# Banks of a skipped branch, its prefetch hint, and the order of the last routed rows

## The chip, the cores and the metric

The kernel runs on one core of a Trainium2 chip. The metric is the device time of one execution, in microseconds (us). Engine names: PE is the matrix engine (TensorE), PEld its weight loads, DVE is VectorE, ACT is ScalarE, POOL is GpSimd, SP is SyncE, which here does nothing but start DMA transfers. An engine takes its instructions in order; engines wait for each other through semaphores.

## The reference

Three parts follow each other: a clustered attention, a mixture of experts, and a bilinear block.

```python
# attention: B, H, S, D = 2, 8, 768, 64; 16 clusters per head
mask = q_assign[:, :, :, None] == k_assign[:, :, None, :]
scores = np.where(mask, scale * np.matmul(q, k.transpose(0, 1, 3, 2)), -1e9)
attn = softmax(scores)                       # over the last axis
x = (attn @ v) as 1536 rows of 512
# mixture of experts: 8 experts, each row goes to the one with the largest logit
expert_idx = np.argmax(logits, axis=1)
for e in range(E):
    h = np.maximum(x[mask] @ w1[e], 0.0)     # 512 -> 1024
    out[mask] = gate_w[mask, None] * (h @ w2[e])
# bilinear
out = ((out @ w_a) * (out @ w_b)) @ w_out    # 512 -> 1536 -> 512
```

## The kernel before

Everything is float32. A product of full precision is made of three passes over numbers split into a high and a low part (`hi`, `lo`): hi by hi, lo by hi, hi by lo. The expert weights come from memory in loads of 512 KB (`raw_0`, `raw_1`, ... on SP, L129, four buffers); ACT writes the high part of each half (L150), DVE the low part (L156), and only when both halves of a buffer are split may SP load into it again.

**Attention.** A loop over 96 steps (`for s in range(nst)`, L753) makes scores, row maxima, exponentials, transposes and the product with v. When a group of rows is done, `route_gen` (L600) finds for each row the expert and its place in that expert's list, and POOL scatters the row into the buffer `xs_d` in memory (L641), 256 places (CAP) for each expert. The work of a group is a generator whose parts are run between the steps.

**The near rows.** The last three tiles of rows (128 each) of the second batch would reach memory too late for expert 0, which is computed first. So expert 0's transposed input `xT_near`, two PSUM tiles, is put together on PE: `near_load` (L676) reads what memory holds of expert 0 into `xe_near`, `near_trans` (L682) transposes that by products with a unit matrix, and `inject(t)` (L688) adds the rows of tile t by 8 products with `oneh`, a matrix of ones and zeros that puts each row in its place (4 column groups, high and low part each). `near_hi` on ACT and `near_lo` on POOL split the rows. Before, the order on PE is inject(0), the place numbers `pos` of the last tile, inject(1), near_trans, the counts `cnt_p`, inject(2). Then ACT and DVE split the result into `xTh` and `xTl` (L901, L903).

**The experts.** From L1171 on a loop runs over steps G. Step G multiplies by a 128-column slice of w1 (`layer1`, 12 products into the PSUM tile `h_G`, which lies in the tag `et0` or `et1` by turns); ACT and DVE make `hh_G` and `hl_G` of it (L1063, L1064); two steps later `layer2(G)` (L1079) multiplies them by w2 into the two tiles `y`: 6 products. In PE's queue that reads h_0, h_1, then the branch below, then h_2, y of 0, h_3, y of 1, h_4, y of 2, and so on. h_G may only start when `hl_(G-2)` has been read out of the same PSUM tag. At f == 5 of each expert PE also transposes the next expert's rows (`trans_x`, L982).

**The branch.** If an expert has more than 256 rows, a branch (`rare`, L1004) computes the others. With these inputs no expert does, so all five engines skip it: each reads the largest count `most` (L1005), compares (L1006), and goes on behind the branch. So that semaphore counts are the same on both ways, the skipped way holds instructions that raise semaphores by what the branch would have (shown as EVENT_SEMAPHORE at L1006). What the branch reads and writes counts as a dependence: `ov_ph` and `ov_py` in it lie in the PSUM tags `et0` and `et1` and are read by DVE, so that h_2 behind it, in `et0`, waits for DVE's semaphore as it stands behind the branch. ACT's first work behind the branch is to start the load of expert 1's rows (`load_xe(1)`, L976), which waits for DMA semaphores that SP raises behind the branch. DVE computes, between the count and the branch, ten small operations on the counts (`ov_s`, `scan`, `ov_i`, L909 to L925), which the branch and later steps read.

L838 marks a place at which a hint for the branch is given, on PE. The program's order is fixed by hand (`manual_schedule`).

Of the kernel before, what the change touches and what calls it, by code (L numbers as in the profile page):

```python
# [9 lines left out]
F32 = mybir.dt.float32  # L10
# [12 lines left out]
P = 128  # L23
# [18 lines left out]
def kernel(  # L42
# [557 lines left out]
    def route_gen(b, t0, n):  # L600
# [10 lines left out]
        if near and t0 > HALF:  # L611
            inject(1)
            near_trans()
        sl = rt.tile([P, HALF, NE], F32, tag="r_sl", name=f"sl_{b}_{t0}", bufs=2)[:, :n]
# [66 lines left out]

    def near_trans():  # L682
        for j in range(DC):
            for t in range(CT):
                nc.tensor.matmul(near_t["ps"][j // 2][:, j % 2, t * P:(t + 1) * P], near_t["xe"][:, t, j * P:(j + 1) * P], ident,
                                 start=False, stop=False)

    def inject(t):  # L688

        if t == 0:  # L690
            near_t["ps"] = [psa.tile([P, 2, CAP], F32, tag="sc", name=f"xT_near_{u}", bufs=2) for u in range(2)]
        for j in range(DC):
            for k_ in ("hi", "lo"):
                nc.tensor.matmul(near_t["ps"][j // 2][:, j % 2, :], near_t[k_][:, t, j * P:(j + 1) * P], near_t["oneh"][:, t, :],
                                 start=(t == 0 and j % 2 == 0 and k_ == "hi"), stop=(t == HALF - 1 and j % 2 == 1 and k_ == "lo"))

# [56 lines left out]
    for s in range(nst):  # L753
# [44 lines left out]
        if pp == NP - 1:  # L798

            if i in (0, 2, 4, 6):  # L800
                split_some(1)
            if 8 <= i < 8 + HALF:
                near_hi(i - 8, 1, 0, 2 * (HP - 1) * D)
                near_lo(nc.gpsimd, i - 8, 1, 0, 2 * (HP - 1) * D)
        if s + 1 == nst or steps[s + 1][0] != g_:
            def then(g=g_):
                pp, t0, n = g
                b, hp = divmod(pp, HP)
                if hp < HP - 1:
                    yield from pv_gen(g)  # L810
                elif pp < NP - 1:
                    yield from pv_gen(g)
                    yield from pick_gen(b, t0, n)
                    yield
                    yield
                    yield from route_gen(b, t0, n)
                elif s + 1 < nst:
                    yield from pv_gen(g, pick_gen(b, t0, n))
                    yield from route_gen(b, t0, n)
                else:  # L820
                    yield from pv_gen(g, pick_gen(b, t0, n), lambda: inject(0))
                    near_hi(HALF - 1, 1, 2 * hp * D, DM)
                    yield from route_gen(b, t0, n)
            work.append(then())
        came = [(g, next(g, 0)) for g in work]
        later = [g for g, r in came if r is True]
        work = [g for g, r in came if r is None]

    work = (later + work)[::-1]
# [7 lines left out]
    inject(HALF - 1)  # L837
    tc.mark_branch_hint_location("rare", "LikelyTaken", engines=[mybir.EngineType.PE])  # L838
    for t in range(NT - HALF + 1, NT):
# [62 lines left out]
    for u in range(2):  # L902
# [5 lines left out]
    ov_s = left.tile([1, NE, OVM], F32, name="ov_s")  # L908
    nc.vector.tensor_tensor(out=ov_s, in0=cnt[0:1].to_broadcast([1, NE, OVM]),  # L909
                            in1=ovt.rearrange("p (o j) -> p o j", o=1).to_broadcast([1, NE, OVM]), op=ALU.is_gt)  # L910

    scan = [left.tile([P, 3 * NE], F32, name=f"scan_{i}") for i in range(2)]
    for t in scan:
        nc.gpsimd.memset(t, 0.0)
    nc.vector.tensor_scalar(out=scan[0][:, NE + 1:2 * NE + 1], in0=cnt[:, :, 0], scalar1=-float(CAP), scalar2=0.0, op0=ALU.add, op1=ALU.max)
    nc.vector.tensor_scalar(out=scan[0][:, 2 * NE + 1:], in0=cnt[:, :NE - 1, 0], scalar1=float(CAP), scalar2=None, op0=ALU.min)
    for i, d in enumerate((1, 2, 4, 8)):
        nc.vector.tensor_add(scan[1 - i % 2][:, NE:], scan[i % 2][:, NE:], scan[i % 2][:, NE - d:3 * NE - d])
    obase, pbase = scan[0][:, NE:2 * NE], scan[0][:, 2 * NE:]

    ov_i = left.tile([1, 4 * NE], I32, name="ov_i")
    nc.vector.tensor_copy(ov_i[:, :2 * NE], scan[0][0:1, NE:])
    with nc.allow_low_precision(reason="whole numbers below 2^24"):
        nc.vector.tensor_reduce(out=ov_i[:, 2 * NE:3 * NE], in_=ov_s, axis=AX.X, op=ALU.add)
    nc.vector.tensor_copy(ov_i[:, 3 * NE:], cnt[0:1, :, 0])  # L925

    psa_stack.close()
    ps_s = ctx.enter_context(tc.tile_pool(name="ps_s", bufs=2 * CT, space=PSUM, reuse_waits="tile"))
    ps_t = ctx.enter_context(tc.tile_pool(name="ps_t", bufs=1, space=PSUM, reuse_waits="tile"))
# [74 lines left out]
    def rare():  # L1004
        n_most = nc.values_load(most, min_val=0, max_val=NTOK)  # L1005
        with tc.If(n_most > CAP, label="rare"):  # L1006
# [3 lines left out]
            xrT = ovb_[:, 2, :].rearrange("p (j t) -> p j t", t=P)  # L1010
            hT = ovb_[:, 3:5, :].rearrange("p a (j t) -> p (a j) t", t=P)
            nc.vector.memset(yr, 0.0)
            n_t = [nc.values_load(ov_i[0:1, 3 * NE + e:3 * NE + e + 1], min_val=0, max_val=NTOK) for e in range(NE)]
# [5 lines left out]
            for e in range(NE):  # L1019
                n_e = nc.values_load(ov_i[0:1, 2 * NE + e:2 * NE + e + 1], min_val=0, max_val=OVM)  # L1020
                row = nc.values_load(ov_i[0:1, e:e + 1], min_val=0, max_val=NTOK)
                with tc.For_i(0, n_e, 1) as it:
                    nc.sync.dma_start(out=xr, in_=xs_d[bass.ds(it * P + e * RX + CAP, P), :])
                    for c in range(FF // 512):
                        for z in range(2):
                            nc.sync.dma_start(out=ovw[c][:, z], in_=chunks[4 * e + 2 * c + z])
                    pt = ps_t.tile([P, DC, P], F32, tag="pp", name=f"ov_pt_{e}")
                    for j in range(DC):
                        nc.tensor.transpose(pt[:, j, :], xr[:, j * P:(j + 1) * P], ident)
                    nc.vector.tensor_copy(xrT, pt)  # L1030
                    for c in range(FF // 512):
                        ph = ps_t.tile([P, 4, P], F32, tag="et0", name=f"ov_ph_{e}_{c}")
                        for f in range(4):
                            for j in range(DC):
                                nc.tensor.matmul(ph[:, f, :], ovw[c][:, 0, j, f * P:(f + 1) * P], xrT[:, j, :], start=(j == 0), stop=(j == DC - 1))
                        nc.vector.tensor_scalar(out=hT[:, 4 * c:4 * c + 4, :], in0=ph, scalar1=0.0, scalar2=None, op0=ALU.max)
                    py = ps_t.tile([P, DM], F32, tag="et1", name=f"ov_py_{e}")
                    for c in range(FF // 512):
# [30 lines left out]
    def layer2(G):  # L1069
# [4 lines left out]
        if f == 0:  # L1074
            ys_ps[e] = [ps_s.tile([P, DM], F32, tag="sc", name=f"y_{e}_{t}") for t in range(CT)]
        for t in range(CT):
# [57 lines left out]
    def bil2(I):  # L1134
# [4 lines left out]
        if f == 0:  # L1139
            o_f[ck] = []  # L1140
            o_ps[ck] = [ps_s.tile([P, DM], F32, tag="sc", name=f"o_{ck}_{t}") for t in range(CT)]
        o_f[ck].append((w[:, :, ff, :], gh, gl))
# [28 lines left out]
    for G in range(total_f + tot + LAG):  # L1171
# [9 lines left out]
        if I < 0:  # L1181
            layer1(G)
            e, f = divmod(G, NF)
            if G == 2 * NF:
                result_rows()
            if G > 3 * NF:
                next(gg, None)
            if f == 5:
                if e + 1 < NE:
                    trans_x(e + 1, xe_t[e + 1])  # L1190
                else:
                    trans_x(("b", 0), x2_t[0])
                if e + 2 < NE:
                    load_xe(e + 2)
# [55 lines left out]
```

## Time and profile before

| | |
|---|---|
| three runs | 816.12, 816.9 (median), 818.7 us |
| the profiled execution | 817.1 us |
| its span, from the first to the last instruction | 815.4 us |
| busy: PE, DVE, ACT, POOL | 784.6, 488.0, 401.1, 96.7 us |
| granted clock of TensorE, mean | 0.988 |

The attention takes the first 290 us of the span, the near rows and the branch the stretch from about 290 to 314, the experts go on to about 470, and the bilinear block is the rest. An engine's busy time says little by itself: an operation that lies beside a busy PE costs nothing. What counts is where PE stands still, and which wait ends last there. Times in views are from the start of the span.

### The profile page before, as it was taken

Reading aid. Unit: us, or ns where it says so; the run is one execution under the profiler, and the core shown is the slowest. Engines: PE = TensorE matmul, PEld = TensorE weight load, DVE = VectorE, ACT = ScalarE, POOL = GpSimd, SP = SyncE. Lnnn points to the kernel's source line nnn. Section 1 sums busy time; section 2 is a strip of 40 time slices with the busy share of each in tenths; the row PEclk is TensorE's granted clock in tenths of the full one; section 3 lists DMA queues with packets and bytes.
Section 4 is the critical chain, followed back from the end, with each engine's and each line's share of the span. In section 5 each row is a group of like instructions: output and inputs, shape, how many; then the busy total and the mean of one; then the engine's idle time right before and its main releaser. Section 6 shows DMA issues by size and latency. Waiting matters only on the chain.

```text
span 815.4 us, 13853 instructions
## 1 busy us (share of the span) xinstructions
PE 784.6 (96%) x5377; PEld 675.9 (83%) x5377; DVE 488.0 (60%) x998; ACT 401.1 (49%) x869; POOL 96.7 (12%) x128
## 2 busy tenths in 40 slices
PE   8899999999999976999999999999999999999997
PEld 5767777777777665999999999999999999999996
DVE  7786676775777764886676699999432222222221
ACT  4666766777656663765555555555221221212211
POOL 5212203224000130000004200000010010010101
PEclk9999999999999997999999999999999999999999
DMA  7137313254120136887778976764010000000000
GB/s 192 43 102 252 78 40 97 53 175 110 31 59 10 68 103 200 300 270 252 227 229 185 239 238 191 249 192 140 1 54 27 27 27 1 1 27 2 27 1 26
DMA packets 45385, 92.60 MB, mean 114 GB/s; under 512 B 6264, under 2 KB 15096, under 8 KB 45312
## 3 DMA queue, kind: packets, MB, share of 16 engines
q1 hardware_dynamic: 41104, 81.67, 34.4%
q0 software_dynamic: 2304, 6.31, 2.1%
q10 hardware_dynamic: 1904, 3.67, 1.4%
q8 instruction: 43, 0.70, 0.4%
q14 instruction: 30, 0.25, 0.1%
HBM read 69.27 MB, written 14.69 MB: 103 GB/s over the span
## 4 chain that ended last, share of the span: by engine, by line
issue 41%; PE 18%; DMA 1%; POOL 1%; POOLq 0%; ACT 0%; SPq 0%
PE h L1001 9%; PE y L1079 8%; DMA tab_d<-id_gate,slot_i 1%; POOL out_dram L1160 1%; PE xT L989 1%; DMA res<-tab_d 0%; POOLq L1245 0%; POOL tick L1165 0%; ACT w L150 0%; ACT hh L1063 0%; POOL tick L889 0%; POOLq L1160 0%; SPq L891 0%
## 5 line engine op out<-in xcount | busy, mean ns | idle before, releaser
L1122 DVE TENSOR_TENSOR ga<-ab,ga 128x256 f32<-128x256 f32 x72 | 30.4, 423 | 151.6 <-ACT ga L1121 151.6
L510 ACT ACTIVATE E<-sc,nmx 128x768 f32<-128x768 f32 x96 | 86.8, 904 | 57.2 <-DVE nmx L505 45.5
L1121 ACT COPY ga<-ab 128x256 f32<-128x256 f32 x72 | 26.8, 373 | 160.6 <-PE ab L1001 160.5
L505 DVE TENSOR_REDUCE nmx<-sc 128x1 f32<-128x768 f32 x96 | 91.4, 953 | 17.2 <-PE sc L497 14.8
L525 PEld LDWEIGHTS et<-ident,E 128*128 128x128 f32 x576 | 63.0, 141 | 35.9 <-ACT E L510 11.4
L1149 PE MATMUL o<-w,gh 128*128 128x512 f32 x288 | 90.6, 396 | 0.0
L525 PE MATMUL et<-ident,E 128*128 128x128 f32 x576 | 83.0, 280 | 5.9 <-ACT E L510 4.3
L156 DVE TENSOR_TENSOR w<-raw,w 128x512 fp32r<-128x512 f32 x128 | 82.5, 686 | 8.3 <-ACT w L150 6.3
L1001 PEld LDWEIGHTS h<-xTh,w 128*128 128x128 f32 x512 | 70.3, 192 | 17.1 <-issue 11.6
L1001 PE MATMUL h<-xTh,w 128*128 128x256 f32 x512 | 72.4, 285 | 11.6 <-DVEq L1006 11.4
L531 DVE COPY ET<-et 128x384 f32<-128x384 f32 x96 | 52.6, 548 | 51.2 <-PE et L525 51.0
L1079 PE MATMUL y<-w,hh 128*128 128x512 f32 x256 | 81.5, 400 | 0.0
L150 ACT CAST w<-raw 128x512 fp32r<-128x512 f32 x128 | 72.8, 620 | 7.9 <-DMA raw<-in_moe_w_dram 7.7
L552 PE MATMUL pv<-ET,v 128*64 128x384 f32 (+2 forms) x408 | 73.0, 479 | 0.6 <-ACT ET L529 0.5
L496 PE MATMUL sc<-K,Q 80*128 80x512 f32 x192 | 73.1, 381 | 0.0
L497 PE MATMUL sc<-K,Q 128*128 128x512 f32 x192 | 61.7, 342 | 0.0
L1063 ACT ACTIVATE hh<-h 128x256 fp32r<-128x256 f32 x64 | 24.6, 384 | 68.1 <-PE h L1001 55.5
L1125 ACT CAST gh<-ga 128x256 fp32r<-128x256 f32 x72 | 29.3, 406 | 56.2 <-DVE ga L1122 56.2
L1149 PE MATMUL o<-w,gl 128*128 128x512 f32 x144 | 56.1, 389 | 0.0
L1149 PEld LDWEIGHTS o<-w,gh 128*128 128x128 f32 x288 | 49.4, 189 | 6.5
L1160 POOL DMA_INDIRECT out_dram<-ot,res x12 | 11.6, 964 | 337.7 <-DVE ot L1159 336.3
L1064 DVE SCALAR_TENSOR_TENSOR hl<-h,hh 128x256 fp32r<-128x256 f32 x64 | 27.0, 422 | 39.1 <-ACT hh L1063 39.1
(284 smaller groups left out, 1535.9 us busy)
## 6 DMA issues: line engine op xcount, KB each, us to landing
raw<-in_moe_w_dram SPq DMA_DIRECT2D x64, 512.0 KB, 4.8
raw<-in_moe_w_a_dram SPq DMA_DIRECT2D x12, 512.0 KB, 3.6
raw<-in_moe_w_b_dram SPq DMA_DIRECT2D x12, 512.0 KB, 3.5
raw<-in_moe_w_out_dram SPq DMA_DIRECT2D x12, 512.0 KB, 3.8
xs_d<-zero SPq DMA_DIRECT2D x8, 512.0 KB, 6.3
ys_d<-ys SPq DMA_DIRECT2D x8, 512.0 KB, 5.1
xe<-xs_d ACTq DMA_DIRECT2D x7, 512.0 KB, 8.3
v<-in_v_dram SPq DMA_DIRECT2D x8, 384.0 KB, 3.0
```

The source lines that it names most:

```text
L150: nc.scalar.copy(hi, w)
L156: nc.vector.tensor_sub(lo, w, hi)
L496: nc.tensor.matmul(ps[:, lo:hi], Q3[:, qs], K3[:, h * S + lo:h * S + hi], start=True, stop=False)
L497: nc.tensor.matmul(ps[:, lo:hi], Q2[:, qs], K2[:, h * S + lo:h * S + hi], start=False, stop=True)
L505: nc.vector.tensor_reduce(out=nmx[pp][:, h, t:t + 1], in_=sc[s], axis=AX.X, op=ALU.max, negate=True)
L510: nc.scalar.activation(e, sc.pop(s), AF.Exp, bias=nmx[pp][:, h, t:t + 1], accum_out=sums[pp][:, t, h:h + 1])
L525: nc.tensor.transpose(pt[:, j * P:(j + 1) * P], e[:, kt * P:(kt + 1) * P], ident)
L531: nc.vector.tensor_copy(dst, src)
L552: nc.tensor.matmul(pv[h * D:(h + 1) * D, :], vt[:, h, kt, :], ets[g, h][:, kt, :n * P], start=(kt == 0), stop=(kt == NT - 1))
L1001: nc.tensor.matmul(ps, s_, m_, start=(i == 0), stop=(i == len(ops) - 1))
L1079: nc.tensor.matmul(ys_ps[e][t], s_[:, t * P:(t + 1) * P], w[:, m_, ff, :], start=(f == 0 and i == 0), stop=(f == NF - 1 and i == 2))
L1149: nc.tensor.matmul(o_ps[ck][t], s_[:, t * P:(t + 1) * P], w_[:, m_], start=(f == 0 and i == 0), stop=(f == NF2 - 1 and j == len(o_f[ck]) - ...
```

## The change

The PSUM tiles of the branch (`ov_pt`, `ov_ph`, `ov_py`) lie in the tag `pp` and in two tags of the y tiles that are next used by expert 1; the pool of the y tiles has one named tag for each of the four places, taken in the same turns as before. The hint's call names no engines. The ten operations on the counts stand in a function `further`, called behind h_1. The transposes of the near rows come first, in PE's transpose mode, and open the PSUM tiles; inject(0) and inject(1) come behind the last tile's place numbers. `near_hi` and `near_lo` of the near rows are called later in the same step. For expert 0 the next expert's transposes come one step later (f == NF - 2 instead of 5).

```diff
         near = b == B - 1 and t0 >= HALF
         if near and t0 > HALF:
-            inject(1)
-            near_trans()
+            for j in range(HALF - 1):
+                inject(j)
...
     def near_trans():
+
+        near_t["ps"] = [psa.tile([P, 2, CAP], F32, tag="sc", name=f"xT_near_{u}", bufs=2) for u in range(2)]
         for j in range(DC):
             for t in range(CT):
-                nc.tensor.matmul(near_t["ps"][j // 2][:, j % 2, t * P:(t + 1) * P], near_t["xe"][:, t, j * P:(j + 1) * P], ident,
-                                 start=False, stop=False)
+                nc.tensor.matmul(near_t["ps"][j // 2][:, j % 2, t * P:(t + 1) * P], near_t["xe"][:, t, j * P:(j + 1) * P], ident, is_transpose=True,
+                                 start=(j % 2 == 0 and t == 0), stop=False)
...
-                                 start=(t == 0 and j % 2 == 0 and k_ == "hi"), stop=(t == HALF - 1 and j % 2 == 1 and k_ == "lo"))
+                                 start=False, stop=(t == HALF - 1 and j % 2 == 1 and k_ == "lo"))
...
             if i in (0, 2, 4, 6):
                 split_some(1)
-            if 8 <= i < 8 + HALF:
-                near_hi(i - 8, 1, 0, 2 * (HP - 1) * D)
-                near_lo(nc.gpsimd, i - 8, 1, 0, 2 * (HP - 1) * D)
...
-                    yield from pv_gen(g, pick_gen(b, t0, n), lambda: inject(0))
+                    yield from pv_gen(g, pick_gen(b, t0, n), near_trans)
...
         work = [g for g, r in came if r is None]
+        if pp == NP - 1 and 8 <= i < 8 + HALF:
+            near_hi(i - 8, 1, 0, 2 * (HP - 1) * D)
+            near_lo(nc.gpsimd, i - 8, 1, 0, 2 * (HP - 1) * D)
...
-    tc.mark_branch_hint_location("rare", "LikelyTaken", engines=[mybir.EngineType.PE])
+    tc.mark_branch_hint_location("rare", "LikelyTaken")
...
-    nc.vector.tensor_tensor(out=ov_s, in0=cnt[0:1].to_broadcast([1, NE, OVM]),
...
+    def further():
+
+        nc.vector.tensor_tensor(out=ov_s, in0=cnt[0:1].to_broadcast([1, NE, OVM]),
...
+        nc.vector.tensor_copy(ov_i[:, 3 * NE:], cnt[0:1, :, 0])
...
-    ps_s = ctx.enter_context(tc.tile_pool(name="ps_s", bufs=2 * CT, space=PSUM, reuse_waits="tile"))
+    ps_s = ctx.enter_context(tc.tile_pool(name="ps_s", bufs=1, space=PSUM, reuse_waits="tile"))
...
+            pt = ps_t.tile([P, DC, P], F32, tag="pp", name="ov_pt")
+            ph = ps_s.tile([P, 4, P], F32, tag=f"sc{CT}", name="ov_ph")
+            py = ps_s.tile([P, DM], F32, tag=f"sc{CT + 1}", name="ov_py")
...
-                        ph = ps_t.tile([P, 4, P], F32, tag="et0", name=f"ov_ph_{e}_{c}")
...
-                    py = ps_t.tile([P, DM], F32, tag="et1", name=f"ov_py_{e}")
...
-            ys_ps[e] = [ps_s.tile([P, DM], F32, tag="sc", name=f"y_{e}_{t}") for t in range(CT)]
+            ys_ps[e] = [ps_s.tile([P, DM], F32, tag=f"sc{e % 2 * CT + t}", name=f"y_{e}_{t}") for t in range(CT)]
...
             layer1(G)
+            if G == LAG - 1:
+                further()
...
-            if f == 5:
+            if f == (5 if e else NF - 2):
                 if e + 1 < NE:
                     trans_x(e + 1, xe_t[e + 1])
```

The second column of these rows is the line, then the operation and output<-inputs, in the order of an engine's queue. PE's first rows before; `pc` and `wps` belong to the set-up:

```order
L1245 UNCONDITIONAL_BRANCH
L1245 BRANCH_PREFETCH_HINT
L264 MATMUL pc<-ident,cent_sb 64x128 x2
L214 LDWEIGHTS ones
L214 MATMUL wps<-ones 128x512
```

and after:

```order
L1249 UNCONDITIONAL_BRANCH
L264 MATMUL pc<-ident,cent_sb 64x128 x2
L214 LDWEIGHTS ones
L214 MATMUL wps<-ones 128x512
L214 LDWEIGHTS ones
```

The hint stood at the start of PE's program. In the changed program PE has none there, and no other engine has one ahead of the branch.

PE at the near rows before (`px` is the last attention product, the 8 products of an inject are cut to the first):

```order
L566 MATMUL px_5_3399<-rmat,xt_5_3373 128x144
L694 MATMUL xT_near_3401<-oneh,x_near_hi 128x256
...
L606 MATMUL pos_5_3421<-cum,ones 128x8
L607 LDWEIGHTS tri
L607 MATMUL pos_5_3421<-oh_all,tri 128x8
L694 MATMUL xT_near_3401<-oneh,x_near_hi 128x256
...
L685 MATMUL xT_near_3401<-ident,xe_near 128x128 x4
L685 MATMUL xT_near_3402<-ident,xe_near 128x128 x4
L836 LDWEIGHTS ones
L836 MATMUL cnt_p<-cum,ones 128x8
```

and after:

```order
L566 MATMUL px_5_3399<-rmat,xt_5_3373 128x144
L687 MATMUL xT_near_3401<-ident,xe_near 128x128 x4
L687 MATMUL xT_near_3402<-ident,xe_near 128x128 x4
L606 LDWEIGHTS ones
L606 MATMUL pos_5_3421<-cum,ones 128x8
L607 LDWEIGHTS tri
L607 MATMUL pos_5_3421<-oh_all,tri 128x8
L693 MATMUL xT_near_3401<-oneh,x_near_hi 128x256
...
L835 MATMUL cnt_p<-cum,ones 128x8
```

The transposes went from behind two injections to the head of the sequence, and the place numbers of the last tile now stand ahead of all three injections.

DVE between the count and the branch, before (`w` are split weights, `hl` the low parts of h_0 and h_1):

```order
L907 TENSOR_REDUCE most<-cnt 1x1
L909 TENSOR_TENSOR ov_s<-cnt,ovt 1x80
...
L925 CAST ov_i<-cnt 1x8
L156 TENSOR_TENSOR w_3505<-raw_2141,w_3505 128x512 x2
L1064 SCALAR_TENSOR_TENSOR hl_3526<-h_3512,hh_3525 128x256
L156 TENSOR_TENSOR w_3505<-raw_2214,w_3505 128x512 x2
L156 TENSOR_TENSOR w_3535<-raw_3086,w_3535 128x512 x2
L1064 SCALAR_TENSOR_TENSOR hl_3556<-h_3542,hh_3555 128x256
L156 TENSOR_TENSOR w_3535<-raw_3192,w_3535 128x512 x2
L156 TENSOR_TENSOR w_3565<-raw_3510,w_3565 128x512
L1005 TENSOR_LOAD most
```

and after:

```order
L906 TENSOR_REDUCE most<-cnt 1x1
L156 TENSOR_TENSOR w_3494<-raw_2141,w_3494 128x512 x2
L1065 SCALAR_TENSOR_TENSOR hl_3515<-h_3501,hh_3514 128x256
L156 TENSOR_TENSOR w_3494<-raw_2214,w_3494 128x512 x2
L156 TENSOR_TENSOR w_3524<-raw_3086,w_3524 128x512 x2
L1065 SCALAR_TENSOR_TENSOR hl_3545<-h_3531,hh_3544 128x256
L916 TENSOR_TENSOR ov_s<-cnt,ovt 1x80
...
L925 CAST ov_i<-cnt 1x8
L156 TENSOR_TENSOR w_3524<-raw_3192,w_3524 128x512 x2
L156 TENSOR_TENSOR w_3564<-raw_3499,w_3564 128x512
L1005 TENSOR_LOAD most
```

The ten operations went behind six of the nine weight splits; all of them still stand ahead of the branch.

## Rows read from the trace of the kernel before

**Rows 1.** PE's waits from 290 us on: waiter, awaited, total, times, longest

```profile
PE h L1001 <- DVEq L1006: 11.4, 1, 11.4
```

**Rows 2.** stretches: length, busy of PE, PEld, DVE, ACT, POOL, clock, DMA, GB/s

```profile
291.00:291.50 0.50, 0.00 (x0) 0.00 (x0) 0.45 (x3) 0.49 (x1) 0.50 (x2) 1.00 0.00 0
293.33:296.75 3.42, 3.42 (x18) 3.42 (x18) 1.01 (x6) 1.77 (x7) 2.36 (x7) 0.50 0.54 212
307.00:317.20 10.20, 3.58 (x15) 3.42 (x16) 1.51 (x3) 1.26 (x3) 0.00 (x0) 0.50 0.59 207
317.30:809.30 492.00, 491.99 (x3379) 456.52 (x3377) 268.74 (x539) 199.57 (x432) 25.56 (x45) 1.00 0.41 124
```

**Rows 3.** chain of waits from 300 to 330 us: start, us, what

```profile
313.62 2.90 PE h L1001 x12
316.51 1.78 PE y L1079 x6
318.29 1.42 PE h L1001 x12
319.70 1.40 PE y L1079 x6
...
325.37 0.87 PE xT L989 x8
```

**Rows 4.** line 1006: engine, operation, count, ns min/median/max, first and last start

```profile
L1006 SPq EVENT_SEMAPHORE  x9: 17/17/17, 313.3 to 314.0; - x9
...
L1006 DVEq EVENT_SEMAPHORE  x2: 21/21/21, 313.4 to 313.6; - x2
L1006 POOLq COMPARE_BRANCH  x1: 53/53/53, 301.1 to 301.1; - x1
L1006 PEldq COMPARE_BRANCH  x1: 1246/1246/1246, 301.1 to 301.1; - x1
L1006 POOLq EVENT_SEMAPHORE  x1: 17/17/17, 303.6 to 303.6; - x1
...
L1006 DVEq COMPARE_BRANCH  x1: 72/72/72, 308.3 to 308.3; - x1
```

**Rows 5.** DMA from 311 to 312 us: queue, kind, packets, MB, share

```profile
q14 instruction: 2, 0.02, 3.9%
```

**Rows 6.** timeline at the branch: start, us, engine, line, operation, shapes [idle before]

```profile
300.41 0.22 DVE L909 TENSOR_TENSOR ov_s<-cnt,ovt 1x80 f32<-1x80 f32 x1
...
302.03 1.28 DVE L156 TENSOR_TENSOR w<-raw,w 128x512 fp32r<-128x512 f32 x2
...
303.33 4.64 SPq L129 DMA_DIRECT2D raw<-in_moe_w_dram  x4
...
313.65 0.47 ACTq L976 DMA_DIRECT2D xe<-xs_d  x1
...
316.55 0.38 ACT L1063 ACTIVATE hh<-h 128x256 fp32r<-128x256 f32 x1 [8.94 <-PE h L1001]
...
316.96 0.42 DVE L1064 SCALAR_TENSOR_TENSOR hl<-h,hh 128x256 fp32r<-128x256 f32 x1 [8.63 <-ACT hh L1063]
```

**Rows 7.** timeline at the near rows, same columns

```profile
292.02 0.38 PE L694 MATMUL xT_near<-oneh,x_near_hi 128*128 128x256 f32 x1 [1.29 <-ACT oneh L629]
...
292.28 0.17 DVE L598 TENSOR_TENSOR oh_all<-cd,cm 128x8 bf16<-128x8 f32 x1
...
292.95 0.28 PE L694 MATMUL xT_near<-oneh,x_near_lo 128*128 128x256 f32 x1
...
294.21 0.28 DVE L674 TENSOR_TENSOR x_near_lo<-xrow,x_near_hi 128x128 fp32r<-128x128 f32 x1
...
297.56 0.37 PE L694 MATMUL xT_near<-oneh,x_near_hi 128*128 128x256 f32 x1
...
298.32 1.07 ACT L901 CAST xTh<-xT_near 128x512 fp32r<-128x512 f32 x2 [3.18 <-PE xT_near L694]
```

**Rows 8.** DMA issues: output<-input, count, KB each, median us to landing

```profile
raw<-in_moe_w_dram SPq DMA_DIRECT2D x64, 512.0 KB, 4.8
```

More of the change, by code (lines that the diff above doesn't have):

```diff
@@ L682, in near_trans @@
     def near_trans():
+        near_t["ps"] = [psa.tile([P, 2, CAP], F32, tag="sc", name=f"xT_near_{u}", bufs=2) for u in range(2)]
         for j in range(DC):
             for t in range(CT):
-                nc.tensor.matmul(near_t["ps"][j // 2][:, j % 2, t * P:(t + 1) * P], near_t["xe"][:, t, j * P:(j + 1) * P], ident,
-                                 start=False, stop=False)
+                nc.tensor.matmul(near_t["ps"][j // 2][:, j % 2, t * P:(t + 1) * P], near_t["xe"][:, t, j * P:(j + 1) * P], ident, is_transpose=True,
+                                 start=(j % 2 == 0 and t == 0), stop=False)
     def inject(t):
-        if t == 0:
-            near_t["ps"] = [psa.tile([P, 2, CAP], F32, tag="sc", name=f"xT_near_{u}", bufs=2) for u in range(2)]
         for j in range(DC):
@@ L914 @@
         nc.gpsimd.memset(t, 0.0)
[L915 to L918, printed above, removed]
     obase, pbase = scan[0][:, NE:2 * NE], scan[0][:, 2 * NE:]
     ov_i = left.tile([1, 4 * NE], I32, name="ov_i")
[L922 to L925, printed above, removed]
+    def further():
+        nc.vector.tensor_tensor(out=ov_s, in0=cnt[0:1].to_broadcast([1, NE, OVM]),
+                                in1=ovt.rearrange("p (o j) -> p o j", o=1).to_broadcast([1, NE, OVM]), op=ALU.is_gt)
+        nc.vector.tensor_scalar(out=scan[0][:, NE + 1:2 * NE + 1], in0=cnt[:, :, 0], scalar1=-float(CAP), scalar2=0.0, op0=ALU.add, op1=ALU.max)
+        nc.vector.tensor_scalar(out=scan[0][:, 2 * NE + 1:], in0=cnt[:, :NE - 1, 0], scalar1=float(CAP), scalar2=None, op0=ALU.min)
+        for i, d in enumerate((1, 2, 4, 8)):
+            nc.vector.tensor_add(scan[1 - i % 2][:, NE:], scan[i % 2][:, NE:], scan[i % 2][:, NE - d:3 * NE - d])
+        nc.vector.tensor_copy(ov_i[:, :2 * NE], scan[0][0:1, NE:])
+        with nc.allow_low_precision(reason="whole numbers below 2^24"):
+            nc.vector.tensor_reduce(out=ov_i[:, 2 * NE:3 * NE], in_=ov_s, axis=AX.X, op=ALU.add)
+        nc.vector.tensor_copy(ov_i[:, 3 * NE:], cnt[0:1, :, 0])
     psa_stack.close()
-    ps_s = ctx.enter_context(tc.tile_pool(name="ps_s", bufs=2 * CT, space=PSUM, reuse_waits="tile"))
+    ps_s = ctx.enter_context(tc.tile_pool(name="ps_s", bufs=1, space=PSUM, reuse_waits="tile"))
     ps_t = ctx.enter_context(tc.tile_pool(name="ps_t", bufs=1, space=PSUM, reuse_waits="tile"))
@@ L1026, in rare @@
                             nc.sync.dma_start(out=ovw[c][:, z], in_=chunks[4 * e + 2 * c + z])
-                    pt = ps_t.tile([P, DC, P], F32, tag="pp", name=f"ov_pt_{e}")
                     for j in range(DC):
@@ L1140, in bil2 @@
             o_f[ck] = []
-            o_ps[ck] = [ps_s.tile([P, DM], F32, tag="sc", name=f"o_{ck}_{t}") for t in range(CT)]
+            o_ps[ck] = [ps_s.tile([P, DM], F32, tag=f"sc{ck % 2 * CT + t}", name=f"o_{ck}_{t}") for t in range(CT)]
         o_f[ck].append((w[:, :, ff, :], gh, gl))
@@ L1192 @@
                     trans_x(("b", 0), x2_t[0])
+            if f == 5:
                 if e + 2 < NE:
```

1 line of the change is left out of this document (removed).

## The prediction

> **What bounds the kernel now.** I read the waits of PE first. From 290 us to the end PE stands still once for long: 11.4 us at the product h (L1001) behind the skipped branch, released by DVE's semaphores of line 1006 [rows 1]. Then the stretches: from 317.3 to 809.3 us PE is busy 491.99 of 492.00 us at full clock [rows 2]. So whatever lets PE take up the experts' steps earlier moves the end by as much, unless PE runs out of weights or inputs later. PE also stands still 1.29 us ahead of the first injection [rows 7], and twice it runs at half the granted clock (1.2 of 2.4 GHz): from 293.33 to 296.75 us, behind that gap, and from 307.0 to 317.2 us, behind the stop at the branch [rows 2].
>
> Line 1006 shows why the branch costs so much. POOL compares at 301.1 us and raises its semaphore at 303.6: 2.5 us. DVE compares at 308.3 and raises at 313.4: 5.1 us; SP's first semaphore comes at 313.3 [rows 4]. A skipped branch is a jump, and the instructions behind it must be fetched. Of the fetches two land between 311 and 312 us [rows 5], behind the four weight loads that SP started from 303.33 to 307.97 us [rows 6]; POOL's came while no load ran. PE compared at 301.1, and its comparison, the one with a hint, took 1.25 us [rows 4]: PE could have gone on at about 302.4, and waited for DVE instead.
>
> **The change: what PE may now do behind the branch.** With ov_ph and ov_py out of the h tags, h_2 waits only for hl_0 and h_3 for hl_1, both ahead of the branch on DVE. So PE does four blocks in the gap: h_2, y of 0, h_3, y of 1, and then stops at h_4, which needs hl_2. That is the new end of the wait: hl_2 is behind the branch on DVE, hh_2 behind it on ACT, and ACT first starts expert 1's row load, which waits for SP to have passed. What is queued behind that load on ACT is every later hh.
>
> Call S the time at which SP and DVE have passed, 313.3 before. Then ACT's load starts 0.35 later (313.65) and takes 0.47; hl starts 0.41 after hh (316.96 against 316.55) and takes 0.42 [rows 6]; with 0.1 for the semaphores h_4 starts at S + 1.75. Before, h_4 started at 319.70 + 1.40 = 321.10 [rows 3]. With S as before that is 315.05, a gain of 6.05 us.
>
> S itself: the ten operations moved behind the first splits took from 300.41 to 302.03, 1.6 us [rows 6]; all else on DVE up to the branch is the same work, so DVE and SP reach the branch when they did. But six splits come 1.6 us earlier, and with them SP's first three of four loads; only the fourth keeps its time. The fetches therefore meet less traffic. The ends are no gain (S = 313.3) and a fetch as quick as POOL's, 308.3 + 2.5 = 310.8, a gain of 2.5. I take 0.9, as three quarters of the loads leave earlier and the fourth still runs: 6.95 us.
>
> From this comes off a clock that falls again. Before, the first blocks behind the stop ran slow: h 2.90 against 1.42, y 1.78 against 1.40, 1.86 us lost [rows 3]. After, the four blocks take 2 x (1.42 + 1.40) = 5.6 us, and PE stops a second time. I take it that the loss is paid again, now on h_4 and the y behind it (bounds 0 and 1.86, or 3 if the next blocks are slow too). Net of the branch: 6.95 - 1.86 = 5.1 us.
>
> **The hint.** The call is meant for all engines, but the order of the program shows that the only hint there was, PE's, is gone and none has come [the order of PE's first rows above]. So PE pays a fetch too: 2.5 us as POOL did at that very time, or 5.1 as DVE did, instead of 1.25. Cover: PE has four blocks of 5.6 us to do before about 314, so a start up to 308 costs nothing; from 301.1 + 5.1 = 306.2 there are two us left, and half a clock during the blocks would use them up. I cost it at nothing. The Trainium skill, Runtime: NRT & Kernel Launch, section Instruction fetch mechanics, says that a taken branch to code that is not loaded waits for a DMA fetch, which speaks against taking a hint away; the trace agrees with its 2.5 and 5.1 us. By that rule PE pays what the others paid; by the contrary, that PE has the target loaded anyway, nothing; only a fetch much longer than DVE's makes a difference, and that is a rival below.
>
> **The near rows.** Before, the third injection starts at 297.56 and ACT's split at 298.32 [rows 7], because the transposes and the second injection stand ahead of it at half clock; its inputs had been ready since 294.21 + 0.28 = 294.5. After: the transposes need xe_near, whose load has ended by 291.0 (no DMA traffic from 291.0 to 291.5 [rows 2]), and 8 passes in transpose mode cost 0.87, as for expert 1 [rows 3]. They end at about 292.0, in a gap that was empty. The place numbers need oh_all, ready at 292.28 + 0.17 = 292.45 [rows 7], so they are not held up, and come before the injections, not behind the first. An injection is 8 products; seven steps from 292.02 to 292.95 give 0.133 each at full clock [rows 7], and 18 products in 3.42 us give 0.19 at half clock [rows 2]. From 292.6 on, at full clock: two injections 2.13, counts 0.1, so the third starts at 294.8 and the gain is 297.56 - 294.8 = 2.7 us. If the clock falls at 293.33 as it did: five products at 0.133, eleven at 0.19, counts 0.1, third injection at 295.6, its first half 0.2 slower: 1.7 us. Ends 1.7 and 2.7; I take 1.7, because PE still does the same injections late in the stretch and the trace shows half clock at this very place. The Trainium skill, TensorE: Matmul & The Clock Gate, Part 4: PE-mode transpose, says that transposes do not count as work for the clock as products do; in this rule the filled gap does not keep the clock up and the gain is 1.7, without it 2.7. The stretch from 293.33 shows only that products alone, with the gap, did not keep it.
>
> At no cost: near_hi and near_lo called later (ACT copies of 0.4 beside PE's products; without that cover 0.4 once), the y tiles' named tags (the same turns), expert 1's transposes one step later (its row load is started some 10 us before they come, against 11.7 before [rows 3, 6]). The load for the next weights starts with hl_2's successors, so weights come later against h_4 than before; the splits are four layer steps ahead, so I cost that at nothing too.
>
> **Sum.** 5.1 + 1.7 = 6.8 us from the profiled execution's 817.1: 810.3. That execution lies 0.2 above the median of 816.9, so 810.1 is the time to compare with the median.
>
> **Rivals.**
> - The clock stays up at one of the two places, or both: 1.0 or 1.86 less, or 2.9: 809.1, 808.2 or 807.2. For it speaks that PE has more to do near both stops; against it that it fell at both. Chance 0.27.
> - The fetch is as quick as POOL's for all: another 1.6 us, 808.5, and 805.6 with a full clock. For it: three loads are out of the way; against: the fourth is not. Chance 0.06.
> - xe_near comes late: the transposes head PE's queue, so the place numbers wait behind them. Rows 2 show quiet DMA from 291.0, so at most the 1.7 are lost: 812. Chance 0.07.
> - PE without its hint is late: fetched only when the loads are through, as DVE was, it goes on at about 313 and the new banks are worth 0.5. With the near rows 817.1 - 1.7 - 0.5 = 814.9, no change that can be told. It decides from a start later than 308. Chance 0.07.
> - Slower: the weights run out. Four buffers, one load for each layer step of 2.82 us [rows 3], so a buffer may take 11.3 us from load to both splits. With the 2.8 us of a step for the splits, PE is starved from a landing time of 8.5 us on; the median is 4.8 [rows 8]. With 9.5 each of some 55 steps is 0.26 longer: 14 us, 824. Earlier steps press harder on the loads, but nothing near twice the landing time is in sight. Chance 0.03.
>
> **How the numbers follow.** The forecast has 0.47, the rivals 0.50, anything else 0.03. A measurement of this kernel can tell 0.3% (2.5 us) from no change, so faster is below 814.5: forecast, clock, quick fetch and late xe_near, with a little off for several small losses at once, 0.88; same 0.09 (the late PE and the rest); slower 0.03. The range holds the forecast, the clock and most of the fetch at its low end, and a late xe_near with a longer slow clock at its high end: 806.3 to 813.3.
>
> **What would show it.** In the profile after: h_2 starts at 304 to 307, less what the near rows gave, and is no longer released by line 1006; PE's long wait is at h_4, on DVE or ACT, and shorter; the third injection starts by 295.7; comparisons on all engines take no hint; the stretch of the experts has PE busy throughout. I am wrong if h_2 still starts behind 311 (PE's fetch), if S has moved later, or if PE stands still for weights or rows in the steps that follow.

## The result, and the profile after

| | before | after |
|---|---|---|
| all runs, median | 817.8 us (4 runs, 816.12 to 818.98) | 808.95 us (4 runs, 808.22 to 810.05) |
| the profiled execution | 817.1 us | 808.22 us |
| its span | 815.4 us | 806.5 us |

The ratio is 0.9894, with a 95% interval of 0.9871 to 0.9918. The forecast was 810.1 us, a ratio of 0.9917 to 816.9: the time lies inside the range that was given, and the gain was sized 2 us too small (6.8 forecast, 8.9 between the two spans).

PE's waits of the changed kernel from 285 us on:

```profile
PE h L1001 <- PEq L1006: 3.1, 1, 3.1
PE h L1001 <- DVE hl L1065: 1.4, 1, 1.4
PE h L1001 <- issue: 0.7, 1, 0.7
PE xT_near L687 <- DMA xe_near<-xs_d: 0.7, 1, 0.7
```

The 11.4 us at h_2 [rows 1] have become two waits: 3.1 us for PE's own passing of the branch, then 1.4 us at h_4 for hl_2. The chain of waits from 310 us on, start and length, shows how h_4 hangs on the others:

```profile
310.62 0.42 ACTq L976
311.03 0.05 issue
311.08 0.39 ACT hh L1064
311.47 0.02 issue
311.50 0.44 DVE hl L1065
311.93 0.04 issue
311.98 1.70 PE h L1001 x12
313.68 1.39 PE y L1080 x6
315.07 1.43 PE h L1001 x12
```

That is the chain that was forecast: ACT's row load, hh_2, hl_2, h_4. Where h_2 ran 2.90 and y 1.78 us behind its stop [rows 3], h_4 takes 1.70 and y 1.39; the next h takes 1.43. Line 1006 (engine, operation, ns, first and last start):

```profile
L1006 SPq EVENT_SEMAPHORE  x9: 17/17/17, 310.3 to 310.9; - x9
...
L1006 DVEq EVENT_SEMAPHORE  x2: 21/21/21, 308.3 to 308.4; - x2
L1006 POOLq COMPARE_BRANCH  x1: 53/53/53, 299.0 to 299.0; - x1
L1006 PEldq COMPARE_BRANCH  x1: 3902/3902/3902, 299.0 to 299.0; - x1
L1006 POOLq EVENT_SEMAPHORE  x1: 17/17/17, 301.5 to 301.5; - x1
...
L1006 DVEq COMPARE_BRANCH  x1: 72/72/72, 305.0 to 305.0; - x1
L1006 SPq COMPARE_BRANCH  x1: 50/50/50, 306.8 to 306.8; - x1
```

Set against [rows 4]: PE's comparison takes 3.90 us instead of 1.25, DVE needs 3.3 us instead of 5.1 to pass, SP 3.5 (306.8 to 310.3) instead of 4.4 (308.9 to 313.3). The stretches, with the columns of [rows 2]:

```profile
293.33:296.75 3.42, 2.72 (x23) 2.48 (x23) 0.96 (x5) 2.56 (x8) 2.50 (x9) 1.00 0.47 184
303.21:306.90 3.69, 3.69 (x15) 3.53 (x16) 2.72 (x10) 0.62 (x1) 0.00 (x0) 0.54 0.89 299
306.90:310.50 3.60, 3.60 (x22) 2.91 (x20) 0.00 (x0) 0.00 (x0) 0.00 (x0) 1.00 0.42 146
311.98:800.00 488.02, 488.02 (x3355) 453.62 (x3356) 267.70 (x538) 198.21 (x431) 25.14 (x44) 1.00 0.41 126
```

The near rows ran at full clock. Behind the branch the clock was at half, 1.2 GHz, for nearly all of the stretch from 303.21 to 306.90 (0.54), while PE did h_2 and part of y; then it was full, and stayed so over the stop at h_4. From 311.98 on PE is busy without a gap.

**Where the 8.9 us come from.** Four marks divide the two profiles: the last two attention products `px`, the starts of h_0 and h_4, and SP's first semaphore. In the timeline of before, then of after:

```profile
290.21 0.51 PE L566 MATMUL px<-rmat,xt 128*128 128x144 f32 x2
...
298.96 1.23 PE L1001 MATMUL h<-xTh,w 128*128 128x256 f32 x8 [0.20 <-ACT xTh L901]
```

```profile
290.44 0.51 PE L566 MATMUL px<-rmat,xt 128*128 128x144 f32 x2
...
296.63 1.53 PE L1001 MATMUL h<-xTh,w 128*128 128x256 f32 x8 [0.70 <-issue]
```

| stretch | before | after | gain |
|---|---|---|---|
| start to px | 290.21 | 290.44 | -0.23 |
| px to h_0: near rows | 8.75 | 6.19 | 2.56 |
| h_0 to SP's semaphore (313.3, 310.3) | 14.34 | 13.67 | 0.67 |
| SP's semaphore to h_4 (321.11, 311.98) | 7.81 | 1.68 | 6.13 |
| h_4 to the end of the span | 494.29 | 494.52 | -0.23 |

The sum is 8.90, the difference of the spans. The table compares single executions; px alone starts anywhere from 289.98 to 292.26 us in the fourteen profiles taken. The experiments are therefore read by intervals from px and h_0. (The h_4 of before is that of the chain [rows 3]; where PE comes to h_4 without a stop, the timeline starts it 0.2 us earlier, 320.94.)

### The profile page after: what moved, and what is told of

It reads as the page before. It is cut to its first block, busy times and chain, and to the rows that moved or that the text cites. A ratio compares the mean times of both kernels' runs of the same rounds, so it can differ in the third digit from the quotient of the medians.

```text
span 806.5 us, 13836 instructions
## 1 busy us (share of the span) xinstructions
PE 781.1 (97%) x5369; PEld 672.6 (83%) x5369; DVE 487.2 (60%) x998; ACT 399.8 (50%) x869; POOL 96.5 (12%) x128
## 4 chain that ended last, share of the span: by engine, by line
issue 41%; PE 17%; DMA 1%; POOL 1%; POOLq 0%; ACT 0%; ACTq 0%; DVE 0%; SPq 0%
PE h L1001 8%; PE y L1080 8%; DMA tab_d<-id_gate,slot_i 1%; POOL out_dram L1161 1%; PE xT L989 1%; DMA res<-tab_d 1%; POOLq L1249 0%; POOL tick L1166 0%; ACT hh L1064 0%; ACT w L150 0%; ACTq L976 0%; DVE hl L1065 0%; POOL tick L888 0%; POOLq L1161 0%; SPq L890 0%
## 5 line engine op out<-in xcount | busy, mean ns | idle before, releaser
L1080 PE MATMUL y<-w,hl 128*128 128x512 f32 x128 | 50.0, 391 | 0.0
```

Of the source, the lines that this page charges most:

```text
L1080: nc.tensor.matmul(ys_ps[e][t], s_[:, t * P:(t + 1) * P], w[:, m_, ff, :], start=(f == 0 and i == 0), stop=(f == NF - 1 and i == 2))
```

## Experiments

The parts measured alone come first. Unless told otherwise, ratios are to the kernel before on the same chip, with their 95% interval.

**The banks alone** (before, with the `ov_` tiles and the y tiles in the tags of the change):

```diff
-                        ph = ps_t.tile([P, 4, P], F32, tag="et0", name=f"ov_ph_{e}_{c}")
+            ph = ps_s.tile([P, 4, P], F32, tag=f"sc{CT}", name="ov_ph")
```

> The kernel before with the other banks alone; the hint on PE, the ten operations and the near rows stay as they were. Theory A (h_4 follows SP's passing of the branch by 1.7 us, whatever PE does before): SP passes at 313.3 as before, h_4 starts at about 315.0 instead of 321.1, a gain of 6.1 us; PE has its hint, is through with its four blocks at about 308.5 and then stands still for more than 6 us, so its clock falls and h_4 and the y behind it pay about 1.6: net 4.5 us, a ratio of 0.9945. Theory B (the clock is only lost once, ahead of h_2, and not again at h_4): 6.1 us, 0.9925. Theory C (the banks gave all of the 8.9 us): 0.989.

Measured: 812.85 us (9 runs), ratio 0.9939 (0.9916 to 0.9963). PE's wait, the chain behind it, and the stretches of its four blocks, of the stop and of h_4:

```profile
PE h L1001 <- DVE hl L1064: 6.8, 1, 6.8
```

```profile
315.25 2.93 PE h L1001 x12
318.18 1.61 PE y L1079 x6
```

```profile
302.58:308.45 5.87, 5.86 (x36) 4.98 (x36) 4.14 (x8) 1.08 (x2) 0.00 (x0) 1.00 0.81 263
308.45:315.25 6.80, 0.00 (x0) 0.00 (x1) 0.42 (x1) 0.89 (x3) 0.00 (x0) 0.74 0.25 93
315.25:319.79 4.54, 4.54 (x20) 4.23 (x21) 4.51 (x9) 3.75 (x8) 0.00 (x0) 0.64 0.84 257
```

Theory A's clock: PE passes at 302.3, does its blocks at full clock, stands still 6.8 us, and h_4 and y then cost 2.93 + 1.61 = 4.54 instead of 2.83, 1.7 us lost. For the clock this is the prediction's picture of the changed kernel, in a kernel in which it holds. The time alone does not tell A from B (0.9925 lies in the interval), and that A's size came out is in part luck: h_4 followed SP's first semaphore (311.2 us) by 4.05 and not by 1.7, because ACT passed at 312.1 and its row load took 1.76 instead of 0.47 us, so that h_4 came 17.84 us after h_0 instead of 22.15, a gain of 4.3 where 6.1 was said; and the near rows, untouched, kept their clock in this profile and gave 1.6.

**The banks alone, with products of ones in the stop:**

```diff
+        if G == LAG + 1:
+            keep_warm(ps_t.tile([P, 512], F32, tag="pv", name="warm_b"), 28)
```

> The kernel before with the other banks alone, and in PE's wait ahead of h_4 28 products of ones into a PSUM tile that nothing reads (some 6 us of work). Theory A (h_4 and the y behind it ran slow, 2.93 and 1.61 us, because PE had stood still 6.8 us): the granted clock stays at 1.00, h_4 takes 1.4 to 1.5 and y 1.4, the end comes 1.6 us earlier than without the products: 811.2, a ratio of 0.992. Theory B (they ran slow because of the weights or the row load beside them): as without, 0.994.

Measured: 812.52 us (5 runs), 0.9933 (0.9909 to 0.9958): by time not told apart from the run without. In the profile the products fill the stop from 311.51 us for 6.22, the wait at h_4 is 1.3 us, and the clock is 1.00 from 306 to 316. The chain:

```profile
319.06 1.69 PE h L1001 x12
```

With the y behind it at 1.39 that is 3.08 instead of 4.54. Theory A holds for the blocks: they ran slow because PE had stood still, not because of the weights. What this is worth in the total stays inside the scatter: the five runs go from 809.83 to 815.33 us, and the profile caught the longest.

**The near rows alone** (before, with the change's order of transposes and injections):

```diff
-            inject(1)
-            near_trans()
+            for j in range(HALF - 1):
+                inject(j)
...
-                    yield from pv_gen(g, pick_gen(b, t0, n), lambda: inject(0))
+                    yield from pv_gen(g, pick_gen(b, t0, n), near_trans)
```

> The kernel before with the new order of the near rows alone. Theory A (what is won ahead of the branch is handed on whole, as all engines and loads move with it): the third injection at about 295.4 instead of 297.56, h_2 at 311.5 instead of 313.6, a gain of 2.1 us, a ratio of 0.9974, and full clock from 293 to 297 us. Theory B (the branch waits for fetches behind the loads, which do not move with PE): h_2 stays at 313 to 313.6, gain 0 to 0.5, ratio 0.9995.

Measured: 817.01 us (12 runs), 0.999 (0.9973 to 1.0007), no change that can be told. Its profile, by itself, reads like theory A: h_2 at 311.54 instead of 313.62. But that profile is of one of five runs of 814.07 to 814.68 us at a mean granted clock of 0.992; the seven others took 816.54 to 817.77 at 0.986 to 0.988. The runs of the kernel before on that chip divide in the same way (five of twenty at 0.992, with 814.58 to 815.14 us), so that at the same clock the new order is worth a few tenths. In which stretch the seven lost their clock no profile shows. The intervals in the other profiles point the same way. From px to h_0 the old order takes 8.75 and 8.72 us in the two profiles in which its clock fell to half, but 7.18 in that of the banks alone, where it stayed at 1.00; the new order takes 6.7 to 6.85 in ten profiles and 6.19 in that of the table, always at 1.00. So in this interval the order is worth some 0.4 us where the clock stays up anyway and 2.0 where it falls, and the profile shown in [rows 2] was one where it fell. Every profile of the new order kept the clock here; whether every run of it did is not shown.

**The ten operations put back in front of the weight splits** (changed kernel otherwise), with the changed kernel once more on the same chip:

```diff
             layer1(G)
-            if G == LAG - 1:
-                further()
...
+    further()
     psa_stack.close()
```

> The changed kernel unaltered, on the same chip as the next three, so that their times can be set against it: 808.5 to 809.5, a ratio of 0.989; from h_0 to h_4 15.0 to 15.5 us, granted clock 1.00 in the near rows, PE's comparison 3.9 to 4.9 us.

> The changed kernel with the ten operations on the counts back in front of the weight splits, all else as changed. Theory A (they are worth the earlier loads, and by these SP's earlier passing, some 0.7 to 0.9 us, on h_4's chain): SP passes about 14.4 us after h_0 instead of 13.7, h_4 starts 0.7 us later, 809.7, a ratio of 0.990. Theory B (the ten operations only changed places, nothing on the chain): as the changed kernel. Theory C (they are what the sum of the two parts measured alone, 0.9939 and 0.999, is short of the whole): 2.5 to 3 us slower, 0.9925.

Measured: the changed kernel 808.78 us (6 runs), 0.9911 (0.989 to 0.9933), from h_0 to h_4 14.96 us; with the operations back 812.48 us (9 runs), 0.9942 (0.9918 to 0.9965). Line 1008 of it, which is the branch there:

```profile
L1008 SPq EVENT_SEMAPHORE  x9: 17/17/17, 311.4 to 312.0; - x9
...
L1008 DVEq EVENT_SEMAPHORE  x2: 21/21/21, 311.6 to 311.7; - x2
...
L1008 DVEq COMPARE_BRANCH  x1: 72/72/72, 306.5 to 306.5; - x1
L1008 SPq COMPARE_BRANCH  x1: 50/50/50, 306.9 to 306.9; - x1
```

DVE needs 5.1 us to pass and SP 4.5, as before the change; in the changed kernel's second profile it was 3.7 and 3.4 (304.9 to 308.6, 306.8 to 310.2). SP reaches the branch at the same time in both. In all unhinted profiles SP takes 3.8 to 4.8 us with the operations in front (five profiles) and 3.2 to 3.7 with them behind (four). So the earlier loads, which are what the move changes for SP, do shorten the fetches, by 1.1 us on SP in this pair, and h_4 comes 16.13 instead of 14.96 us after h_0. That is theory A's mechanism, and theory C's size: 3.7 us between the medians, 2.5 by the two ratios, whose intervals just overlap. The profile caught the fastest of the nine runs (809.41 us, granted clock 0.997); the eight others took 810.85 to 814.08 at 0.990 to 0.995. A clock that falls once more in those runs, behind a stop at h_4 that is longer than the profile's 2.0 us, would fit in part; but runs of the two kernels at the same mean clock still lie 0.5 to 3.1 us apart, and no profile shows it, so it stays open.

By the ratios the parts measured alone are worth 5.0 (banks), 0.8 (near rows) and 2.5 us (ten operations), 8.3 together where the whole is 8.7, with an interval of some 2 us to either side of each. Nothing of a clear size is left for the parts that were not tried alone, the later `near_hi` and `near_lo` and expert 1's transposes one step later.

**The hint given back to PE** (changed kernel otherwise):

```diff
-    tc.mark_branch_hint_location("rare", "LikelyTaken")
+    tc.mark_branch_hint_location("rare", "LikelyTaken", engines=[mybir.EngineType.PE])
```

> The changed kernel with the hint on PE given back. Theory A (the end hangs on h_4, that on SP, and the lost hint only moved PE's idle time): PE's comparison takes 1.25 instead of 3.90 us, h_2 starts at about 300.5 instead of 303.2, h_4 still at 312.0, but PE now stands still some 5 us in one piece ahead of h_4, its clock falls, and h_4 and y pay about 1.6 us: 1.3 to 1.6 us slower than the changed kernel, 810.4, a ratio to before of 0.991. Theory B (the clock does not fall there): as the changed kernel, 0.9894. Theory C (PE's fetch stood in the way of the others): SP passes up to 1 us earlier, 0.988.

Measured: 810.41 us (6 runs), 0.9916 (0.9895 to 0.9938). The number is theory A's, but the profile is not:

```profile
L1006 PEldq COMPARE_BRANCH  x1: 4029/4029/4029, 299.7 to 299.7; - x1
```

PE's comparison took as long as without a hint, and h_4 came 14.95 us after h_0, as in the changed kernel (15.35 and 14.96). The test of the clock that it was meant to be didn't take place; on two chips the times (0.9916, 0.9894) are not told apart.

**The hint on all five engines, and on all but PE:**

```diff
+    tc.mark_branch_hint_location("rare", "LikelyTaken", engines=[mybir.EngineType.PE, mybir.EngineType.Activation, mybir.EngineType.DVE, mybir.EngineType.Pool, mybir.EngineType.SP])
```

> The changed kernel with the hint named for all five engines, so that each has it at its program's start. Theory A (what an engine loses at the branch is the fetch, and a hint takes it away as it did for PE): DVE passes at about 306.3 instead of 308.3, SP at 307.1 to 308.1 instead of 310.3; h_4 starts at 308.8 to 309.8 instead of 312.0, 2.2 to 3.2 us faster if the clock stays up, 0.6 to 1.6 if it falls ahead of h_4: 805.8 to 808.3, a ratio of 0.985 to 0.9885. Theory B (a hint this early is forgotten, or the fetch is not what takes the time): as with PE's hint alone, 0.9894 to 0.991.

> The changed kernel with the hint on ACT, DVE, POOL and SP, and none on PE. Theory A (the hint does nothing for PE: its comparison took 3.77, 4.03 and 3.62 us with it and 3.90 without, with the same order of the near rows): as with all five hints, PE's comparison 3.6 to 4.0 us, 806.8, a ratio of 0.987. Theory B (PE's hint is worth something): PE passes later than 303.7, 0.5 to 1.5 us slower than with all five.

Measured with all five: 806.78 us (5 runs), 0.9871 (0.9848 to 0.9893). Line 1006:

```profile
L1006 SPq EVENT_SEMAPHORE  x9: 17/17/17, 307.4 to 310.2; - x9
...
L1006 DVEq EVENT_SEMAPHORE  x2: 21/21/21, 306.2 to 306.3; - x2
...
L1006 PEldq COMPARE_BRANCH  x1: 3622/3622/3622, 299.1 to 299.1; - x1
...
L1006 DVEq COMPARE_BRANCH  x1: 84/84/84, 305.2 to 305.2; - x1
L1006 SPq COMPARE_BRANCH  x1: 70/70/70, 306.9 to 306.9; - x1
```

SP passes in 0.5 us instead of 3.5, DVE in 1.0 instead of 3.3, ACT and POOL in 0.5. The Trainium skill, Runtime: NRT & Kernel Launch, section Instruction fetch mechanics, says that a taken branch waits for the fetch of code that is not loaded; these rows agree, with about 3 us on SP. Nothing stops PE at h_4 now (310.31 us, 13.36 after h_0); what is left is PE's own passing and the slow clock behind it.

Measured without PE's hint: 808.98 us (4 runs), 0.9892 (0.9871 to 0.9913); PE's comparison 4.61 us, h_0 to h_4 15.47. It speaks for theory B, by an interval that overlaps, and the profile is of the longest of the four runs; the last pair tells more.

**The row load behind h_3** (changed kernel otherwise):

```diff
             rare()
-            load_xe(1)
...
             layer1(G)
+            if G == LAG + 1:
+                load_xe(1)
```

> The changed kernel with expert 1's row load called behind h_3 instead of ahead of h_2, so that ACT makes hh_2 before it starts the load. Theory A (h_4's last link is that load, which waits for SP): hh_2 as soon as ACT has passed (308.0) and h_2 is done, hl_2 by 309.0, so h_4 follows y of 1 without a stop at 310.5 instead of 312.0: 1.4 to 1.7 us faster than the changed kernel, about 807.3, a ratio to before of 0.9875. Theory B (DVE's passing or the weights hold h_4 too): at most 0.3 us faster, 0.989.

Measured: 807.91 us (5 runs), 0.988 (0.9861 to 0.9899), a gain over the changed kernel that is not clear of the scatter. The stop at h_4 is gone, as theory A has it, but in this profile PE's comparison took 4.93 us and the half clock lasted past 310 us, so that h_4 came 16.02 us after h_0: PE's own passing had taken the load's place. The profile caught the longest of the five runs (810.79 us), so it does not stand for the median.

**The branch behind h_2, all five hints; then the row load behind h_3; then without PE's hint:**

```diff
         if G == LAG:
-            rare()
-            load_xe(1)
         if I < 0:
             layer1(G)
+            if G == LAG:
+                rare()
+            if G == LAG + 1:
+                load_xe(1)
```

> The changed kernel with the hint on all five engines and the branch one product later, behind h_2. Theory A (PE's passing hangs on something that comes at 302.3 to 303.7 whatever PE did before, as in all profiles so far): PE passes at about 303, has stood still only 1 to 1.5 us since h_2, keeps its clock, and h_4 starts 2.8 (y, h_3) + 1.4 later, at 307.3 instead of 310.3: 803.8, a ratio of 0.9835. Theory B (PE's fetch starts with its comparison and takes 3.6 us from there): PE passes at about 305, after a stop of 3 us, the next blocks run slow again, h_4 at 310 to 311: 806 to 807.5, no gain.

> The branch behind h_2 with all five hints, as in the run before, and expert 1's row load behind h_3. Theory A (the stop of 1.25 us ahead of h_5 came from hh_3 standing behind the load and three casts on ACT): PE goes on without a stop from y of 0, the end comes 1.3 to 1.9 us earlier than with the load in its old place: 804.3, a ratio of 0.984. Theory B (then DVE's splits or the weights hold h_5): 806, 0.986.

> As the kernel before it, with no hint on PE. Here nothing but PE's own passing of the branch stands between h_2 and y of 0, so that what the hint is worth on PE is seen whole. Theory A (nothing; the spread of 3.6 to 4.9 us of its comparison is the load traffic): same time within 0.3 us, PE passes 5.5 us after h_0. Theory B (PE's hint saves a fetch as on the others, 0.7 to 1.1 us by the comparisons so far): PE passes 6.2 to 6.6 us after h_0 or later, and if the longer stop drops its clock another 1 to 1.5 us: 805 to 807.

Measured: branch behind h_2 (load_xe(1) right behind the branch) 805.99 us (4 runs), 0.9861 (0.9838 to 0.9885): PE stood still 1.0 us at the branch and kept its clock, and h_4 came 9.97 us after h_0, but h_5 then waited 1.25 us for hl_3 behind the load and three casts on ACT; less gain than theory A's 803.8. With the load behind h_3: 804.59 us (5 runs), 0.986 (0.9837 to 0.9883), that wait gone, h_4 9.63 us after h_0. Against 0.9911 for the changed kernel on that chip this is clearly faster; from the version before it (0.9861, another chip) it can't be told apart. The same without PE's hint: 808.32 us (6 runs), 0.9901 (0.988 to 0.9921). PE's comparison in these two, the hinted one first:

```profile
L1006 PEldq COMPARE_BRANCH  x1: 1006/1006/1006, 300.5 to 300.5; - x1
```

```profile
L1006 PEldq COMPARE_BRANCH  x1: 4623/4623/4623, 300.7 to 300.7; - x1
```

and the chain of the one without:

```profile
305.63 2.90 PE y L1080 x6
308.53 2.56 PE h L1001 x12
```

On one chip, in kernels that differ in nothing else, PE's hint is worth 3.7 us. At the comparison it is 3.6, and with the slow clock behind the longer stop h_4 comes 15.55 instead of 9.63 us after h_0; the hinted kernel gives back 1.3 us of that later (its h_4 is 6.1 us earlier, its span 4.8 shorter), where its chain of waits goes by the weight loads:

```profile
301.05 5.83 DMA raw<-in_moe_w_dram
...
309.77 3.94 DMA raw<-in_moe_w_dram
```

So theory B, and larger than it said; and the weights, the prediction's slower rival, begin to bind only here. Where the branch stands behind h_1 with the new order of the near rows, PE's comparison took 3.62 to 4.03 us with the hint in three profiles and 3.61 to 4.93 without it in five; in the two old-order profiles with other banks 2.5 and 2.6 with it.

The DMA rows tell more of it. PE's instructions come on a queue of their own, q8, in packets of 16 KB, and in all fourteen profiles PE passes the branch 1.3 to 1.5 us after such a packet has landed. How long the comparison seems to take is set by when that packet starts: 1.2 to 1.3 us ahead of the comparison where it took 1.0 to 1.6 us, 0.2 behind it where it took 2.5 and 2.6, and 1.0 to 2.2 behind it where it took 3.6 to 4.9. In the pair above both kernels start one packet at 299.2 and 299.4 us. With the hint PE passes on that one. Without it a second one comes, at 302.87, inside the comparison; from 300.70 to 305.30 us:

```profile
q8 instruction: 1, 0.02, 1.3%
```

From 300.50 to 301.60 us, over the hinted comparison, there is none. In the new order with the branch behind h_1 the one packet of the hinted kernels started 1.0 us behind the comparison, as in the changed kernel without a hint, so the hint bought no earlier start there. Three of the five without it took a second packet, none of those with it did. What starts the first packet no run shows.

## Why the prediction was right or wrong

The time came out in the forecast range, and of the 2.1 us by which the gain was sized too small 1.6 are the clock at h_4 and 0.9 the near rows; the other terms take 0.4 back. One of the rivals came true in place of the forecast's own clock: the clock stayed up at both places, for which 807.2 was said, and it fell at a third, h_2, where the wait hid it.

- **The new end of the wait: right.** h_4 was to start at S + 1.75; it started 1.68 behind SP's semaphore, a gain of 6.13 where 6.05 was said. One sign was not: PE's longer wait is not at h_4 (1.4 us) but at h_2, for its own passing (3.1).
- **S earlier by 0.9: right in mechanism and nearly in size** in the profile (0.67; 1.1 on SP's passing when the operations alone are put back). SP, which passed last, came to the branch 10.2 us after h_0 instead of 9.9 and passed 0.9 us faster. DVE did not come when it did, as was said, but sooner (8.4 instead of 9.3 us after h_0); the chain goes by SP. By the medians the ten operations are worth more, 3.7 us, and the rest of that is not explained.
- **The clock falls again at h_4, 1.86 us: the step that failed.** It did not fall there: the granted clock is 1.00 from 306.90 us on, and h_4 and y lose 0.3 (1.70 + 1.39 instead of 2.83), as h_4 did at full clock in the kernel with products of ones (1.69). The prediction let PE do its four blocks at full clock and then stand still long; the banks alone show that this would have cost 1.7. In the changed kernel PE passed late, at 303.0, the half clock fell on h_2 and y of 0, whose time was covered by the wait at h_4, and the second stop was 1.4 us and not the 6.8 of the banks alone. In the other profiles with a stop of 1.2 to 2.0 us ahead of h_4 or h_5 the clock stayed up as well. The two costs that were put at nothing, the fetch and the slow blocks, were hidden as said; what was missed is that they also shortened the next stop.
- **The near rows: 1.7 forecast, 2.56 between the two profiles.** "PE still does the same injections, and the trace shows half clock at this very place" failed: the clock was full in all eleven profiles of the new order. But the old order kept it too in one of three, so that the two profiles overstate the part; alone it could not be told from nothing. So the 2.56 is in part a lucky draw. The step of 0.19 at half clock mixed the injections' products, which took 0.21, with the shorter transposes; that moves the lower end by some 0.2. The rule in the Trainium skill, TensorE: Matmul & The Clock Gate, Part 4: PE-mode transpose, that transposes do not count as work for the clock in the way products do, is neither borne out nor refuted: the clock stayed up with and without them.
- **The hint costed at nothing: right for this kernel.** PE passed at 303.0, before the 308 from which it would have cost, though after 3.9 us and not 2.5. The other half was right as well: the call hints no engine, as the comparisons of 299 to 307 us show beside those of the hinted kernel. What acted were the banks, the ten operations and the near rows; a hint was not in the program.
- **The other rivals did not decide.** PE waited 0.7 us for xe_near, inside a gap that was there before; PE is busy 488.02 of 488.02 us from h_4 to 800 us. The chances named for faster add up to 0.87, so 0.88 is a slip; it decides nothing.

## What to carry to other kernels

A branch that nobody takes was paid here by each engine at its fetch, and the engine that passed last set the end for all whose inputs crossed it: look which engine's semaphores the waiting instruction counts, move the work that needs nothing of it in front, and give each engine's hint by name, then look in the program that it is there, and in the trace that the fetch starts ahead of the comparison. Where an engine gets work earlier but the end of its wait stays, ask what the longer second stop does to its clock. And one profile of each kernel is one draw: measure from marks close to the change, and let several profiles say whether a slow stretch belongs to the code.

## What the runs showed of the hardware that was not expected

- A hint at the start of the program, 300 us ahead of the branch, still worked on SP, ACT, DVE and POOL: 0.5, 0.5, 1.0 and 0.5 us to pass in the kernel with all five hints, against 3.5, 3.7, 3.3 and 2.5 in the changed one.
- An unhinted fetch cost DVE and SP 3.2 to 5.1 us here, more where the weight loads came later: 1.1 us on SP for loads started 1.7 us later, in one pair of profiles.
- PE passed the branch 1.3 to 1.5 us after a 16 KB packet on its own instruction queue had landed, in all fourteen profiles; in the one pair of kernels that differ in PE's hint alone, it changed which packet that was.
- An issue of the row load on ACT took 1.76 and 1.86 us in the two profiles with the old order and other banks, 0.42 to 0.77 in all others; why is open.
